# An adaLN block with sliding-window attention and a gated MLP: identity products in a row, another order of all engines' steps, and a last tile in three pieces

## The chip, the cores and the metric

The kernel runs on one core of a Trainium2 chip. The metric is device time in microseconds, from the launch to the end on that core. Engines in the views: PE (TensorE products), PEld (its weight loads), DVE (VectorE), ACT (ScalarE), POOL (GpSimd), SP (SyncE, which here only issues DMAs). Line numbers such as L1166 are those of the kernel before.

## The reference

The input x is 2048 rows of 448 values, in bfloat16. Six vectors of 448 come from one small product, and they shift, scale and gate two blocks:

```python
mod = (silu(c) @ w_mod).reshape(1, 6, 1, 448)
sa, ca, ga, sb, cb, gb = ...                       # six vectors of 448
h = layernorm(x) * (1 + ca) + sa
x = x + ga * A(h)                                  # attention, 16 heads of 28, window of 256 keys, softmax, then @ wo
h = layernorm(x) * (1 + cb) + sb
z = gelu(h @ w_in)                                 # 1792 wide: z1 and z2 of 896
g = w_sp @ layernorm(z2) + b_sp                    # a 2048 x 2048 product over the rows
x = x + gb * ((z1 * g) @ w_out)
```

## The kernel before

x lies in SBUF as 16 tiles of 128 rows (t or j, 0 to 15), worked on in quarters of four tiles (tb, 0 to 3). `hT` is the normalised activations transposed, so that features lie on partitions.

The work in its rough order of time:

- **Head.** Loads of x, c, the first part of w_mod and of wqkv; memsets; `ident`, a 128 x 128 identity made on POOL. `t_cT` (L517) turns c into a column, ACT applies silu. `t_mA` (L557, opened by one product at L561) is the modulation's first two vectors: three steps, each waiting for its own rows of w_mod (`t_wmA`, three loads, L412), 8, 16 and 8 products of one column each. `mod_out` (L569, L570) brings them to `modT`. The transposes of the first quarter (L708), their scaling with `modT` (L715 on ACT, L717 on DVE), and the Q and K products of the first quarter (L756) follow; L840 is V.
- **Identity products.** `warm` (L575 to L583) makes steps that multiply `ident` with itself into a free PSUM bank, 128 x 512, one product each. Nothing reads the result. Of the 54 steps that it offers, the order takes ten.
- **Attention**, tiles 0 to 15: scores (L942, L968, L977), exp on ACT (L929), masks on DVE (L984, L1004), the product with V (L1011), division (L1025, L1027), a DMA transpose, the product with wo (L1035; wo was multiplied with ga on POOL, L605), the residual (L1040), statistics (L621, L624, L626, L629, L633, L636), the second layer norm (`norm`, L641 on DVE or L646 on POOL, with a 64-column copy, L649 or L650), a DMA transpose to hT and its scaling (L1058, on ACT, DVE or POOL). For the quarters 2 and 3 the first layer norm goes the same way (L646, L692, L697 to L700); Q and K products of the quarters 1 to 3 are L798, their evictions L807 to L810, V's L843 to L846.
- **Gated MLP.** z2 (L1097) and z1 (L1143), gelu on ACT, layer norm of z2; the row product with w_sp (L1166, 28 groups of 16 products), a DVE step that adds b_sp (L1170), a POOL step that multiplies with z1 (L1173), the product with w_out (L1185), the residual (L1195), the store (L1200).

All of this is one list of steps. Each step names the engines that could run it, with a duration for each (for a product or a vector step, in us), what it depends on, and what buffer it takes. The order isn't computed when the kernel is built: `ORDER` (L19) is a written list of words such as `317.v` or `57.p.1` (step number, engine, buffer slot). `Sched.order` reads it: each engine executes its steps in the order of the list, and takes the engine and slot named there. The durations and landing times in the code, with `HOP`, `NEXT`, `PEL`, `SHAPE` and `TURN`, give only planned times; those decide in which sequence a step's semaphore waits are written (L234), and nothing else. `Sched.waits` then puts a semaphore wait ahead of each step for the dependences that its engine doesn't already know of; PE needs none for dependences on PE itself.

The step behind each word in the head of PE's queue: 46 is L517; 57 to 62 and 71 to 77 are identity products; 54, 55, 56 are the three steps of the modulation; 158 and 161 are L708; 170 is the first step of L756.

Of the kernel before, what the change touches and what calls it, by code (L numbers as in the profile page):

```python
# [9 lines left out]
HOP = 0.12  # L10

NEXT = {"dve": 0.08, "act": 0.11, "pool": 0.045}
# [7 lines left out]
2.a 25.v 35.g 0.s 26.v 27.v 28.v 38.g 39.g 3.a 4.s 36.g 45.a 33.g 29.v 5.s 30.v 31.v 37.g 32.v 40.g 6.s 7.s 41.g 8.s 140.v 141.v 57.p.1 58.p.2 46.p.0  # L20
48.a 47.a 59.p.3 60.p.4 54.p.1 61.p.5 62.p.6 55.p 34.g 142.g 49.a 56.p 134.v 135.v 136.v 143.g 137.g 138.g 144.v 145.a.0 139.a.1 71.p.7 72.p.3 158.p.2
50.g 126.a 127.v 111.v 112.v 159.v 161.p.3 160.a 162.a 163.a 128.g 42.g 1.s 9.s 10.s 130.a 131.g 11.s 12.s 13.s 14.s 15.s 16.s 152.v 129.v 153.v 154.v
146.v 155.g 132.v 147.v 148.v 149.g 133.g 156.v 73.p.0 74.p.6 170.p.4.5 171.p.6.7 172.p 173.p 174.p 175.p 178.p 176.p 177.p 184.p.0.1 185.p.2.3 186.p
187.p 188.p 189.p 193.p 179.p 192.p 181.a 182.a 150.v 151.v.2 197.v 157.a.3 183.a 167.p.5 164.p.6 191.p 218.p.3 190.p 168.v 169.a 195.a 165.v 166.v
194.v 200.p.7 226.v 230.v 227.v 219.a 180.a 196.a 204.a 201.p.5 198.p.6 202.v 232.v 231.v 228.v 229.v 233.v 53.v 205.a 199.p.1 203.a 378.p.0 209.p.0
220.p.7 224.p.6 206.p.1 379.a.0 384.p.0 225.a 44.g 51.g 213.v 52.v 43.g 234.g 235.g 210.a 385.a.1 207.p.0 211.a 221.a 380.v 382.v 236.v 239.g.0
237.v.1 113.p.1 238.v.2 115.v 240.v.3 114.v 403.p.0 117.p.0 388.v 118.v 244.p.1 208.p.6 404.a.2 405.a 212.a 245.v 386.v 241.p.0 410.p.0 222.p.7
381.p.0 383.p 214.s 217.s 216.s 215.s 17.s 24.s 20.s 18.s 22.s 120.s 119.s 21.s 19.s 246.a 242.v 243.v 411.a.3 249.p.1 223.a 412.a 250.a 247.p.0 248.a
430.p.0 432.p.0 387.p 389.p 431.a.4.0 275.v 279.v 281.v 277.v 282.v 280.v 278.v 276.v 283.g 326.v 284.g 390.v 391.v.0 285.v 332.v 413.v 406.v 408.v
287.v.0 415.v 434.v 288.g.1 292.s 291.s 253.p.1 261.p.0 254.a 438.p.0 262.a 439.a.5.1 265.p.1 407.p.0 259.p.0 409.p 266.a 260.a 459.p.0 460.a.6.2  # L30
433.a 251.p.1 414.p 267.p.0 416.p 467.p.0 468.a.0.3 328.v 289.v.2 293.s 286.v.3 330.v 252.v 435.v 290.s 268.v 417.v 418.v.1 329.v 263.p.1 440.p.0
273.p.0 441.a 264.a 257.s 256.s 121.s 258.s 255.s 392.s 419.s 436.p.0 488.p.0 464.v 333.v 327.v 331.v 442.v 443.v 489.a.1.4 437.p 444.p 271.p.1
461.p.0 445.p 463.v 334.g 471.v 274.v 446.v 447.v.2 272.v 462.a 296.a 294.g 297.g 295.g 335.g 496.p.0 497.a.2.0 269.p.0 469.p.0 465.p.0 466.p 298.p.1
470.a 517.p.0 299.a 270.v 336.v 493.v 500.v 490.p.0 300.p.0 473.p 316.p.1 472.v 492.v 301.v 518.a.3.1 521.v 317.v 491.a 525.p.0 498.p.0 474.p
526.a.4.2 475.v 476.v.0 530.v 340.v.0 529.v 501.v 522.v 124.g 337.g.1 125.g 339.g.2 122.g 338.g.3 123.g 448.s 341.s 343.s 342.s 477.s 344.s 318.p.0
312.p.1 494.p.0 319.a 313.a 499.a 546.p.0 302.p.0 519.p.0 495.p 420.p.1 502.p 547.a.5.3 554.p.0 520.a 555.a.6.4 303.v 551.v 421.v 503.p 527.p.0
304.p.0 310.p.1 504.v 505.v.1 559.v 558.v 422.v 305.a 528.a 575.p.0 576.a.0.0 393.p.0 548.p.0 523.p.0 524.p 531.p 532.p 583.p.0 394.v 550.v 345.v
533.v 580.v 534.v.2 549.a 311.a 584.a.1.1 314.p.0 315.v 478.p.1 556.p.0 552.p.0 479.v 346.v 116.s 306.s 506.s 309.s 307.s 535.s 308.s 557.a 604.p.0
449.p.0 553.p 560.p 561.p 577.p.0 605.a.2.2 578.a 612.p.0 613.a.3.3 423.v 588.v 587.v 579.v 450.v 562.v 507.p.1 585.p.0 480.v 395.v 563.v.0 508.v
347.g 348.g 324.p.0 581.p.0 325.a 586.a 633.p.0 634.a.4.4 351.p.1 606.p.0 320.p.0 582.p 607.a 321.a 641.p.0 642.a.5.0 608.v 509.v 609.v 396.v 451.v  # L40
452.v 481.v 397.g 453.g 398.g 482.g 454.g 510.v 617.v 424.v 352.v 589.p 590.p 614.p.0 591.v 536.p.0 616.v 322.p.1 537.v 592.v.1 646.v 511.v 399.v
637.v 400.v.0 401.g 455.g 425.g 615.a 323.a 662.p.0 663.a.6.1 355.p.0 610.p.0 635.p.0 611.p 618.p 619.p 636.a 356.v 670.p.0 671.a.0.2 538.v 620.v
638.v 621.v.2 349.p.1 643.p.0 353.p.0 639.p.0 644.a 350.a 691.p.0 564.s 402.s 666.v 645.v 675.v 622.s 593.s 692.a.1.3 664.p.0 640.p 647.p 648.p
# [224 lines left out]
def bass_adaLN_cond__sliding_block__mixer_gmlp__prompt_kernel(  # L268
# [111 lines left out]
    bM = View(banks, [(6,), (7,)])  # L380
    bA = View(banks, [(6,), (7,), (0,), (1,), (2,), (3,), (4,), (5,)])
    bF = View(banks, [(0, 1), (2, 3), (4, 5), (6, 7)])
    bG = View(banks, [(b,) for b in range(8)])
    MMS = 512 / 2400.0 + 0.003
    MMD = 448 / 2400.0 + 0.003
    PEL = 0.2


    dsem = []

    def load(name, eng, mb, fn, deps=(), prio=0.0, land=None, least=2.9):
        dsem.append(name)
# [876 lines left out]
```

## Time and profile before

| | |
|---|---|
| median of 3 runs | 276.64 us (275.81 to 276.93) |
| the profiled execution | 277.14 us, of which the span of its instructions is 275.2 us |
| busy, PE / DVE / ACT / POOL | 264.7 / 159.3 / 138.2 / 117.6 us |
| L1166, the product with w_sp, on PE | 97.3 us in 437 recorded products |
| L984, masks on DVE | 38.7 us, 56 of 0.723 us |
| L929, exp on ACT, the 2048-wide form | 53.2 us, 28 of 1.900 us |
| L646, layer-norm scaling on POOL / L641, the same on DVE | 1.103 / 0.433 us each |
| DMA | 26.41 MB in 66386 packets |

[...] A few product records are missing in the trace, which can look like a gap of one product's spacing.

### The profile page before, as it was taken

The numbers are of one execution on the slowest core, as the hardware profiler recorded it, in microseconds if no ns is written. First come the engines' busy times: TensorE is split into PE (matmuls) and PEld (weight loads), VectorE is DVE, ScalarE is ACT, GpSimd is POOL, SyncE is SP. The second block draws the span as 40 slices with busy tenths as digits, with TensorE's granted clock in tenths as the row PEclk, the third lists the DMA queues.
The fourth block names the chain that finished last, engine by engine and source line by source line (L and its number), as shares of the span: only waits on it lengthen the run. The fifth ranks groups of instructions, "written<-read, shape, count | busy, mean of one in ns | idle before, by whom it ended". The sixth has DMA issues, their size and how long they took to land.

```text
span 275.2 us, 7464 instructions
## 1 busy us (share of the span) xinstructions
PE 264.7 (96%) x3221; PEld 143.6 (52%) x3246; DVE 159.3 (58%) x370; ACT 138.2 (50%) x189; POOL 117.6 (43%) x172
## 2 busy tenths in 40 slices
PE   5999999899999999999999999999999999999995
PEld 1766565566676866445444444444444444444552
DVE  5599999999999999779365202100331042233343
ACT  5689999899998999889998400000000000000000
POOL 8531229720364694364799105000853053425110
PEclk9999999999999999999999999999999999999999
DMA  7958953551156746937999999100000000002022
GB/s 204 288 190 202 306 104 74 68 77 37 21 61 114 111 67 103 172 60 114 175 196 187 187 198 204 44 0 0 2 0 0 0 2 0 0 0 86 16 92 76
DMA packets 66386, 26.41 MB, mean 96 GB/s; under 512 B 56881, under 2 KB 65266, under 8 KB 66354
## 3 DMA queue, kind: packets, MB, share of 16 engines
q1 hardware_dynamic: 66080, 25.48, 46.7%
q8 instruction: 25, 0.41, 0.6%
q10 hardware_dynamic: 274, 0.46, 0.5%
q14 instruction: 7, 0.06, 0.1%
HBM read 9.07 MB, written 1.84 MB: 40 GB/s over the span
## 4 chain that ended last, share of the span: by engine, by line
PE 77%; DVE 9%; POOL 4%; DMA 4%; issue 2%; SPq 2%; ACT 2%; POOLq 0%
PE ps L1166 35%; PE ps L1097 8%; PE ps L1185 8%; PE ps L1143 8%; PE ps L1011 4%; PE ps L1035 3%; PE ps L968 3%; DVE PT L984 2%; DMA x_sb<-in_A_x_dram 2%; PE ps L756 2%; PE ps L840 2%; POOL xn L646 2%; DMA wmod<-in_w_mod_dram 2%; POOL wo_g L605 1%; DVE st_all L621 1%
## 5 line engine op out<-in xcount | busy, mean ns | idle before, releaser
L929 ACT ACTIVATE PW<-ps 128x2048 bf16<-128x2048 f32 (+1 forms) x56 | 67.5, 1260 | 4.1 <-PE ps L968 3.4
L1173 POOL TENSOR_TENSOR z1T<-tmpg,z1T 128x512 bf16<-128x512 bf16 x28 | 31.8, 1152 | 77.8 <-DVE tmpg L1170 77.8
L1170 DVE TENSOR_TENSOR tmpg<-ps,bsp_bc 128x512 bf16<-128x512 f32 x28 | 19.1, 690 | 73.9 <-PE ps L1166 48.7
L1166 PE MATMUL ps<-wspB,z 128*128 128x512 bf16 x217 | 49.0, 379 | 0.4
L1166 PE MATMUL ps<-wspA,z 128*128 128x512 bf16 x220 | 48.3, 379 | 0.3 <-issue 0.2
L984 DVE TENSOR_TENSOR PT<-PW,mask 128x1024 bf16<-128x1024 bf16 x56 | 38.7, 723 | 0.1
L1166 PEld LDWEIGHTS ps<-wspA,z 128*128 128x128 bf16 x224 | 21.8, 98 | 26.6 <-issue 0.4
L1166 PEld LDWEIGHTS ps<-wspB,z 128*128 128x128 bf16 x224 | 21.9, 98 | 26.1
L1011 PEld LDWEIGHTS ps<-Vaug,PT 128*128 128x128 bf16 x496 | 22.3, 96 | 4.4 <-DVE o_sb L1027 0.5
L1011 PE MATMUL ps<-Vaug,PT 128*128 128x32 bf16 x496 | 24.4, 177 | 0.1
L629 POOL TENSOR_TENSOR rs_all<-ve_all,neghalf 128x1 f32<-128x1 f32 (+1 forms) x31 | 20.0, 650 | 9.3 <-DVE ve_all L626 8.7
L1185 PE MATMUL ps<-w_out_g,z1T 128*128 128x448 bf16 (+1 forms) x119 | 22.3, 341 | 0.0
L1097 PE MATMUL ps<-w_in,hT 64*128 64x448 bf16 x224 | 22.2, 349 | 0.1
L1143 PE MATMUL ps<-hT,w_in 64*128 64x512 bf16 x196 | 21.8, 376 | 0.0
L1011 PE MATMUL ps<-Vaug,PW 128*128 128x32 bf16 x224 | 20.4, 176 | 0.0
L1195 DVE TENSOR_TENSOR fin<-ps,x_sb 128x448 bf16<-128x448 f32 (+1 forms) x17 | 9.8, 593 | 17.2 <-PE ps L1185 17.2
L621 DVE BATCH_NORM_STATS2 st_all<-x_sb 128x6 f32<-128x448 bf16 x32 | 19.1, 613 | 0.5 <-DMA x_sb<-in_A_x_dram 0.5
L798 PE MATMUL ps<-hT,WQK 128*128 128x512 bf16 x66 | 17.2, 379 | 2.1 <-DVE rec_all L1025 0.7
L1011 PEld LDWEIGHTS ps<-Vaug,PW 128*128 128x128 bf16 x224 | 17.6, 96 | 2.4
L626 POOL TENSOR_SCALAR ve_all<-mv_all 128x1 f32<-128x1 f32 (+1 forms) x16 | 4.8, 297 | 31.5 <-DVE mv_all L624 30.9
L1185 PEld LDWEIGHTS ps<-w_out_g,z1T 128*128 128x128 bf16 x119 | 11.6, 98 | 10.0
L1151 ACT ACTIVATE z1T<-ps 128x512 bf16<-128x512 f32 x28 | 14.5, 608 | 4.2 <-PE ps L1143 4.0
(125 smaller groups left out, 370.6 us busy)
## 6 DMA issues: line engine op xcount, KB each, us to landing
out_dram<-fin SPq DMA_DIRECT2D x15, 112.0 KB, 1.7
x_sb<-in_A_x_dram SPq DMA_DIRECT2D x3, 448.0 KB, 5.8
wmod<-in_w_mod_dram SPq DMA_DIRECT2D x1, 1344.0 KB, 9.0
w_in<-in_B_w_in_dram SPq DMA_DIRECT2D x1, 1344.0 KB, 7.7
QBD<-qT SPq DMA_DIRECT2D x16, 64.0 KB, 2.2
w_out_g<-in_B_w_out_dram SPq DMA_DIRECT2D x1, 784.0 KB, 5.8
bsp_bc<-in_B_b_sp_dram SPq DMA_DIRECT2D x1, 512.0 KB, 4.6
x_sb<-in_A_x_dram SPq DMA_DIRECT2D x2, 224.0 KB, 3.9
```

The costliest lines, as they stand in the source:

```text
L621: st = [dve(0.62 if True else 0, lambda e, t=t, ci=ci, s=s: e.bn_stats(st_all[:, slot, t, ci, :], s()), deps(t), prio) for ci, s in enumer ...
L629: rs = pool(0.41 + 0.155 * len(tiles), lambda e: e.tensor_tensor(rs_all[:, slot, a:b], ve_all[:, slot, a:b], neghalf[:, 0:b - a], ALU.pow) ...
L798: m = pe(4 * MMS, [lambda e, h=h, g=g, kc=kc, tb=tb: e.matmul(ps[:, h.slot[0], :], lhsT=WQK[:, kc, 4 * g:4 * g + 4, :].rearrange("p a b -> ...
L929: ex = act(xdur, lambda e, out_ap=out_ap, in_ap=in_ap: e.activation(out_ap(), in_ap(), ACT.Exp, scale=SCALE), [s], v - 8.0 + u, takes, tab ...
L984: return dve(0.70, lambda e: e.tensor_tensor(cols(hp.slot[0] * 2048 + 1024 * k, [[256, 4], [128, 2], [1, 128]]), cols(at_w() + 128 + 192 * ...
L1011: fns.append(lambda e, hp=hp, hO=hO, hi=hi, bi=bi, kb=kb, hd=hd, nb=nb, a=at[hi][bi], p_of=p_of: e.matmul(ps[:, hO.slot[0], 32 * hd:32 * h ...
L1097: return lambda e, kc, p0, start, stop: e.matmul(ps[:, hs[t % 2].slot[hf], 0:D], lhsT=hT[p0:p0 + 64, kc, t * 128:(t + 1) * 128], rhs=w_in[ ...
L1143: return lambda e, kc, p0, start, stop: e.matmul(ps[:, hs[b // 2].slot[b % 2], :], lhsT=w_in[p0:p0 + 64, kc, ft * 128:(ft + 1) * 128], rhs ...
L1166: m = pe(16 * MMS, [lambda e, h=h, si=si, ft=ft, tb=tb: e.matmul(ps[:, h.slot[0], :], lhsT=z2[:, si, ft * 128:(ft + 1) * 128], rhs=(wspA i ...
L1170: a = dve(0.7, lambda e, h=h, ht=ht, tb=tb: e.tensor_tensor(tmpg[:, ht.slot[0], :], ps[:, h.slot[0], :], bsp_bc[:, tb * 512:(tb + 1) * 512 ...
L1173: u = pool(1.16, lambda e, ht=ht, ft=ft, tb=tb: e.tensor_tensor(z1T[tb][:, ft, :], tmpg[:, ht.slot[0], :], z1T[tb][:, ft, :], ALU.mult), [ ...
L1185: return [lambda e, ft=ft: e.matmul(ps[:, h.slot[0], c0:c1], lhsT=z1T[t // 4][:, ft, (t % 4) * 128:(t % 4 + 1) * 128], rhs=w_out_g[:, ft, ...
```

## The change

Four things are changed in the text:

1. `ORDER` is another list. It has 1191 words for 1184. All steps of before are in it; new are three more identity products (75, 76, 77) and four steps of the new last piece (1228 to 1231). Steps per engine: PE 340 to 345, DVE 370 to 356, ACT 172 to 170, POOL 168 to 185, SP 134 to 135.
2. The planned durations, distances and landing times are others (`HOP`, `PEL`, `NEXT`, `land`, `tail` and the like). They change no instruction.
3. The last tile (15) is written in three pieces of 224, 112 and 112 columns, instead of two of 224.
4. The last tile's first product step names all earlier w_out products as dependences (`others`). These are PE steps too, so no wait comes of it.

PE's queue up to the first Q product, in words of the list:

```
before: 57 58 46 59 60 54 61 62 55 56 71 72 158 161 73 74 170 171 ...
after:  46 57 58 59 60 61 62 54 55 56 71 72 73 161 158 74 75 76 77 170 171 ...
```

The end of the list:

```
before: ... 1112.p 1175.p | DVE ... 1185 1179 1113 1176 | SP ... 1186 1180 1114 1177
after:  ... 1175.p 1220.p 1221.p 1224.p 1225.p 1228.p 1229.p | DVE ... 1185 1176 1226 1230 1222 | SP ... 1177 1227 1231 1223
```

(1220 to 1223 are the first piece of tile 15: six products, one product, the residual, the store; 1224 to 1227 the second, 1228 to 1231 the third. 1175 to 1177 are tile 8.)

The diff, with the list and most of the durations left out:

```diff
-HOP = 0.12
+HOP = 0.055
-NEXT = {"dve": 0.08, "act": 0.11, "pool": 0.045}
+NEXT = {"dve": 0.08, "act": 0.12, "pool": 0.045}
...
 ORDER = """
-2.a 25.v 35.g 0.s 26.v ... 57.p.1 58.p.2 46.p.0 ...
+... 57.p.2 58.p.3 59.p.4 60.p.5 61.p.6 62.p.7 54.p.1 55.p 56.p 144.g 145.a.0 50.a ... 71.p.0 72.p.3 73.p.4 161.p.2 158.p.3 ...
...
-    PEL = 0.2
+    PEL = 0.34
...
-    t_c = load("d_c", "act", 0.01, lambda e: e.dma_start(c_row[:], c[0:1, :]), prio=-98.98, land=2.9)
+    t_c = load("d_c", "act", 0.01, lambda e: e.dma_start(c_row[:], c[0:1, :]), prio=-98.98, land=1.6, least=1.5)
...
-        op = add({"pe": (dur, fns)}, deps, prio, take, lat=PEL)
+        op = add({"pe": (dur, fns)}, deps, prio, take, lat=0.2 if shape == "rows32" else PEL)
...
+    others = []
...
-            for c0, c1 in ((0, D // 2), (D // 2, D)) if t == NT - 1 else ((0, D),):
+            for c0, c1 in ((0, D // 2), (D // 2, 3 * D // 4), (3 * D // 4, D)) if t == NT - 1 else ((0, D),):
...
-                m = pe(k * one_mm, outs_of(range(k)), [us[:k], t_woutg], v + 0.01 * (c0 > 0), [h])
+                m = pe(k * one_mm, outs_of(range(k)), [us[:k], t_woutg] + (others if t == NT - 1 else []), v + 0.0001 * c0, [h])
                 if k < 7:
-                    m = pe(one_mm, outs_of([6]), [us, m], v + 0.05 + 0.01 * (c0 > 0))
+                    m = pe(one_mm, outs_of([6]), [us, m], v + 0.02 + 0.0001 * c0)
                 hf = Hold(fiR)
+                others.append(m)
```

More of the change, by code (lines that the diff above doesn't have):

```diff
@@ L420, in bass_adaLN_cond__sliding_block__mixer_gmlp__prompt_kernel @@
     LO, HI, BOTH = slice(0, D), slice(D, 2 * D), slice(0, 2 * D)
[L421 to L423 removed]
+    t_c = load("d_c", "act", 0.01, lambda e: e.dma_start(c_row[:], c[0:1, :]), prio=-98.98, land=1.6, least=1.5)
+    t_wmA = [head("d_wmAa", "act", wmod, w_mod, 0, 2, BOTH, -98.97, 5.0, least=4.2), head("d_wmAb", "sp", wmod, w_mod, 2, 1, BOTH, -98.97, 4.1, least=3.4),
+             head("d_wmAc", "sp", wmod, w_mod, 3, 64, BOTH, -98.96, 5.5, least=3.8)]
     t_wq = []
[L425 removed]
+    for k, (n, cols, at) in enumerate((("q", LO, (5.8, 6.6, 6.8)), ("k", HI, (8.1, 8.9, 9.1)))):
         a, b, c_ = [head("d_w%s%s" % (n, p), "sp", wq_st, A_wqkv, first, rows, cols, -98.95 + 0.03 * k + 0.004 * i, at[i], (), 3.9)
```

159 lines of the change are left out of this document (78 added, 81 removed).

## The prediction

> **What bounds the kernel now.** I read the page first, then the table of stretches, the chain and waits of TensorE, the timeline of the first 20 us, and at last the end.
>
> ```profile
> PE 264.7 (96%) x3221; PEld 143.6 (52%) x3246; DVE 159.3 (58%) x370; ACT 138.2 (50%) x189; POOL 117.6 (43%) x172
> PE   5999999899999999999999999999999999999995
> DVE  5599999999999999779365202100331042233343
> ```
>
> PE has work in nearly every slice; DVE is as full until about 108 us. The stretches put numbers to it (columns: us, then busy time and instructions of PE, PEld, DVE, ACT, POOL; clock; DMA share; GB/s):
>
> ```profile
> 0.00:10.00 10.00, 6.69 (x55) 3.07 (x56) 5.24 (x19) 5.21 (x9) 7.43 (x20) 1.00 0.86 235
> ...
> 18.00:50.00 32.00, 30.67 (x619) 18.65 (x625) 30.44 (x73) 31.34 (x38) 14.55 (x16) 1.00 0.73 156
> 50.00:54.00 4.00, 3.20 (x69) 2.16 (x72) 3.97 (x6) 3.38 (x6) 3.65 (x3) 1.00 0.34 64
> 54.00:108.00 54.00, 53.13 (x1400) 36.79 (x1403) 53.47 (x118) 50.56 (x51) 24.45 (x40) 1.00 0.46 71
> 108.00:154.00 46.00, 45.81 (x456) 21.77 (x458) 31.49 (x93) 38.77 (x70) 30.22 (x58) 1.00 0.90 153
> 154.00:272.00 118.00, 117.32 (x556) 55.24 (x565) 27.83 (x45) 2.99 (x6) 33.67 (x30) 1.00 0.21 47
> ```
>
> From 18 to 154 us PE idles 1.33 + 0.80 + 0.87 + 0.19 = 3.19 of 136 us. PE's useful work is the same before and after the change, so the end can move only by what happens before PE's first useful product, by these 3.19 us or new ones like them, and by the 3.2 us behind PE's last product. Two waits are more than a third of the 3.19:
>
> ```profile
> 50.23 0.81 PE L798 MATMUL ps<-hT,WQK 128*128 128x512 bf16 x3 [0.74 <-DVE rec_all L1025]
> ...
> 53.70 0.93 PE L1035 MATMUL ps<-wo_g,hT 128*128 128x448 bf16 x4 [0.42 <-POOL wo_g L605]
> ```
>
> The first waits for a bank that a busy DVE empties late, the second for the last of four scalings of wo on POOL. Now the head:
>
> ```profile
> 2.39 1.03 PE L578 MATMUL ps<-ident 128*128 128x512 bf16 x2 [2.39 <-POOL ident L498]
> 3.36 0.37 PE L517 MATMUL ps<-one,c_row 1*128 1x1 bf16 x4
> 3.66 1.04 PE L578 MATMUL ps<-ident 128*128 128x512 bf16 x2
> 5.62 0.19 PE L561 MATMUL ps<-xn,ident 128*128 128x8 bf16 x1 [0.92 <-DMA wmod<-in_w_mod_dram]
> ...
> 6.87 0.93 PE L557 MATMUL ps<-sc_sb,wmod 128*128 128x1 bf16 x24
> 7.66 1.01 PE L578 MATMUL ps<-ident 128*128 128x512 bf16 x2
> 8.47 1.06 PE L708 MATMUL ps<-ident,xn 128*128 128x128 bf16 x8
> ```
>
> The ten identity products (L578) lie in pairs between the steps that are needed. Their spacing is 0.427 us, against 0.216 for the same shape later (L1166): the clock is low here. It rises at about 11.58 us, inside the first useful products (by L756 alone):
>
> ```profile
> 10.17:11.46 1.29, 1.28 (x7) 0.91 (x7) 1.00 0.75 192
> 11.62:14.04 2.42, 2.42 (x25) 2.15 (x22) 1.00 1.01 328
> ```
>
> Seven starts in 1.28 us are 0.213 apart; behind 11.6 they are 0.109 apart. (The clock column's 1.00 is no record here.)
>
> **Part 1, the head.** Before: pair, L517, pair, L561 with the first eight of L557, pair, the rest of L557, pair, L708, pair, L756. After: L517 first, then six identity products in a row, all of the modulation, three, L708, four, L756: thirteen for ten. I walk it with the landings of this trace. ident is ready at 2.39; c_row has landed by then (landing record 2.08), so L517 goes ahead at next to no cost. Six products take 2.56 us, to about 4.95. The modulation still waits for its weights: 5.62, then the 6.87 at which the next part landed, then a third that ends at 7.66, since the loads and their queues stand as before. So PE now idles about 0.7 + 1.0 us where one pair used to fill the second gap; nothing needed is later by that. DVE's modT step, which stood behind a WQK copy until 8.64, can go at about 7.85, but that is hidden: PE has 7 identity products queued between 7.66 and L756. With the low clock: 7.66 + 3 x 0.427 + 0.85 (L708) + 4 x 0.427 = 11.5 for the first L756 product, against 10.18. The products needed for it (hT by DVE and ACT, two at 9.4 and 9.8 plus 0.4 to 0.6 each) are ready by 11.1. If the clock rises at 11.58 again, the seven products that ran low now run full, 7 x 0.104 = 0.70 back. Net +1.33 - 0.70 = **+0.63**. The two ends: the clock is up before 7.7 (then L756 starts at 9.6 at full rate, 10.18 + 0.70 - 9.61 = **-1.27**), or it rises later (below).
>
> [...]
>
> **Part 2, the order from 18 to 154 us.** The new constants issue nothing; they gave another order. Counting steps that change engines up to the modulation of hT, at the page's means: layer-norm scalings, net four from DVE (0.433) to POOL (1.103), DVE -1.73, POOL +4.41; hT scalings of L1058, DVE -3 x 0.439, ACT -0.80, POOL +3.99; those of L697, ACT +0.82, POOL -1.03; clearing QBD, DVE -0.91, ACT +1.06; evictions, seven ACT to DVE and four back, DVE +1.85, ACT -1.99; small steps, DVE -0.54, POOL +1.37. Sum: DVE **-2.65**, ACT -0.91, POOL **+8.74** us. DVE idles only about 2 us of 18 to 108, POOL about half of it, so the load goes where room is. What is worth anything is PE's 3.19 us. The eviction that the 0.74 waited for (the last K group of the third quarter) moves from DVE, where masks stand ahead of it, to ACT. The first L1035 stands 17 PE steps further back (step 127 instead of 110), several us of work, while POOL reaches the last wo scaling at about 53 by my count of its queue: the 0.42 goes. I take 0.74 + 0.42 = **-1.1** after rounding; what is late next is the many 0.1 us waits on masks, which I leave. Ends: -2.5 (all but a fifth of 3.19) and +1.5 (the last rival). On SP, x's last quarter is loaded directly behind the third (it lands at 28.9 now, released DVE's stats after a 0.5 us wait), part of wo goes behind the copies of q, hidden since POOL takes it up at 47 or later. From 154 us on, PE has 118 us of queued products, last weights land before (150.8 by the landing records, 154 needed), and one more wspB transpose ahead of them is offset by a wspA transpose issued earlier: nothing.
>
> **Part 3, the end.** Now a full-width tile is last: PE, then 0.62 on DVE, 0.03, SP's issue of 0.33, landing.
>
> ```profile
> 271.95 0.62 DVE L1195 TENSOR_TENSOR fin<-ps,x_sb 128x448 bf16<-128x448 f32 x1 [0.70 <-PE ps L1185]
> ```
>
> After, tile 15 is last in 224 + 112 + 112 columns. The wait list `others` is PE on PE and costs no semaphore. PE streams the same columns. But DVE's order is second piece, third piece, then the first and widest. Widths 448 and 224 cost 0.625 and 0.392, so 112 is estimated at 0.28: the third starts 0.2 behind the last product as now, the first starts 0.19 later and ends at 0.2 + 0.19 + 0.39 = 0.78, against 0.2 + 0.625 = 0.83. SP issues three transfers of 0.33 in line with that. Half the bytes in the last one: **0**, ends -0.2 and +0.2.
>
> **Sum.** +0.63 - 1.1 + 0 = -0.5. The profiled execution took 277.14 (span 275.2 and 1.94 around it) and would be 276.6; the median of the three runs is 276.64, so I say **276.1**. The spread of those runs (275.81 to 276.93) is what a clock rising 2 us earlier or later makes.
>
> **The rivals.**
> - *The row raises the clock early*, before L756 and its seven identity products. For: 2.56 us without a gap, where before no stretch that long came ahead of 5.62. Against: nearly 1.7 us of idling follows. 276.64 - 1.27 - 1.1 = 274.3.
> - *The clock rises later.* It rose 5.96 us after PE's last wait ended (5.62); that distance from 6.87 gives 12.8, and each us of low clock costs half: +0.6. 276.7. [...]
> - *POOL's scalings become the wait* (slower). In the third quarter three of the four scalings are on POOL in series, 3 x 1.103 = 3.3 us, where one was; the transposes to hT come behind the last. Before, hT was complete at 43.1 and PE's L798 took it at 43.9, so only 0.8 us is spare. For: that spare is small. Against: of the three hT scalings that POOL did then (3.07 us) two go to DVE. It decides once DVE gives POOL its statistics about a us later than the 31.6 I count; then PE stalls by 1.5, and the gain of part 2 is spent: 276.64 + 0.63 + 1.5 = 278.8.
>
> **How the numbers follow.** Forecast 0.36, early clock 0.30, late clock 0.12, POOL 0.22. Half a per cent, 1.4 us, is about what a measurement of this kernel can tell from no change. Faster by more: 0.28 of the early clock and 0.04 of the forecast's lower part, 0.32. Slower by more: 0.20 of the POOL case and 0.02 of late clock, 0.22. Same: 0.46. The range for 8 in 10 runs from just below the early clock's 274.3 to 278.5; the forecast's own is 275.2 to 277.3.
>
> **What would show it.** Right: thirteen L578 products, six from about 2.4; L557's second part still waiting until its landing; L756 starting between 9.6 and 11.5 and its spacing telling the clock; no PE wait over 0.3 us at 50 and 54; DVE's last step 224 wide. Wrong: idle of PE between 18 and 154 above 3.2 us, an L798 that waits for hT near 44, or a PE queue that ends with more than 3.3 us to go.

## The result, and the profile after

| | before | after |
|---|---|---|
| median | 276.64 us, 5 runs (275.81 to 276.93) | 280.82 us, 5 runs (280.22 to 281.23) |
| profiled execution, span | 277.14, 275.2 us | 280.22, 278.5 us |

The ratio is 1.0153 (95% interval 1.0134 to 1.0172): slower by about 4.2 us. The prediction was 276.1 us with a range to 278.5, so it was wrong, and in sign. (Two more runs of before have come to the three given above; the median is the same.)

The busy times of the page, to be read against those of before: PE has 35 products more on record (ten are really new, 25 were missing in the trace of before), DVE 2.7 us less, POOL 7.6 us more.

```profile
PE 267.7 (96%) x3256; PEld 144.7 (52%) x3256; DVE 156.6 (56%) x356; ACT 138.1 (50%) x187; POOL 125.2 (45%) x189
```

So the work moved from DVE to POOL as the prediction counted. The table of stretches (us, then busy time and instructions of PE, PEld, DVE, ACT, POOL; clock; DMA share; GB/s) says what it did to PE:

```profile
18.00:50.00 32.00, 30.61 (x622) 18.27 (x620) 29.55 (x71) 30.53 (x35) 12.17 (x13) 1.00 0.66 145
50.00:54.00 4.00, 3.42 (x84) 1.97 (x86) 4.00 (x5) 2.24 (x3) 3.90 (x3) 1.00 0.50 97
54.00:108.00 54.00, 53.41 (x1378) 36.18 (x1377) 52.88 (x111) 50.51 (x50) 28.16 (x45) 1.00 0.40 65
108.00:154.00 46.00, 45.27 (x470) 22.17 (x468) 28.66 (x82) 39.05 (x69) 35.52 (x72) 1.00 0.90 157
154.00:158.00 4.00, 2.00 (x17) 0.74 (x13) 0.94 (x2) 2.56 (x5) 2.27 (x3) 1.00 0.99 180
```

PE idles 1.39 + 0.58 + 0.59 + 0.73 + 2.00 = 5.29 us of these 140, against 3.25 of the same 140 in before (3.19 up to 154). The single waits, from PE's timeline (start, length, what, and in brackets the idle time ahead of it with its releaser):

```profile
49.62 0.93 PE L840 MATMUL ps<-wv,hT 128*128 128x448 bf16 x4 [1.13 <-DVE qT L809]
52.45 0.19 PE L1011 MATMUL ps<-Vaug,PT 128*128 128x32 bf16 x1 [0.45 <-DVE o_sb L1027]
55.10 1.04 PE L798 MATMUL ps<-hT,WQK 128*128 128x512 bf16 x4 [0.59 <-DVE qT L809]
157.30 0.39 PE L1167 MATMUL ps<-wspA,z 128*128 128x512 bf16 x1 [2.00 <-DVE z L1134]
```

(In the kernel after, L1166, L1170, L1173, L1185 and L1195 of before are L1167, L1171, L1174, L1186 and L1197.) The two waits that the prediction wanted gone, at 50.23 and 53.70, are gone. Three others on DVE stand in their place, and a wait of 2.0 us has appeared where before had none, ahead of the product with w_sp.

The best account is by five stretches of PE, cut at the starts of first products: to the first L942; from there to the first L1097 (attention); to the first L1166 (z, the gated MLP's input); to the last product (gating); and from there to the end of the span. Profiled executions, us:

| | head | attention | z | gating | end |
|---|---|---|---|---|---|
| before | 17.66 | 90.44 | 45.75 | 117.71 | 3.64 |
| after | 16.53 | 92.96 | 47.81 | 117.88 | 3.33 |
| difference | -1.13 | +2.52 | +2.06 | +0.17 | -0.31 |

(The first L1166 of before is missing in its record; its weight load puts it at 153.85, which the table uses.) The sum is +3.3 us, as the spans say. The loss is in two places, about half in each: attention and z.

The head of after, for the prediction's walk:

```profile
2.38 2.74 PE L578 MATMUL ps<-ident 128*128 128x512 bf16 x6
5.67 0.80 PE L557 MATMUL ps<-sc_sb,wmod 128*128 128x1 bf16 x24 [0.32 <-DMA wmod<-in_w_mod_dram]
10.12 2.07 PE L756 MATMUL ps<-hT,WQK 128*128 128x256 bf16 x16
```

The row is there, and the second part of L557 waits for its landing, as said. But that landing came at 5.67, not at 6.87, and L756 began at 10.12, with the full clock 0.3 us later (granted clock 1 from 10.44 by the clock's own record; 11.58 in before).

### The profile page after: what moved, and what is told of

It is laid out like the page before. It is cut to its first block, busy times and chain, and to the rows that moved or that the text cites. A ratio compares the mean times of both kernels' runs of the same rounds, so it can differ in the third digit from the quotient of the medians.

```text
span 278.5 us, 7512 instructions
## 1 busy us (share of the span) xinstructions
PE 267.7 (96%) x3256; PEld 144.7 (52%) x3256; DVE 156.6 (56%) x356; ACT 138.1 (50%) x187; POOL 125.2 (45%) x189
## 4 chain that ended last, share of the span: by engine, by line
PE 80%; POOL 7%; DVE 6%; ACT 2%; DMA 2%; issue 1%; ACTq 0%; DVEq 0%
PE ps L1167 35%; PE ps L1186 8%; PE ps L1097 7%; PE ps L1011 6%; PE ps L1035 4%; PE ps L968 4%; PE ps L840 4%; PE ps L798 4%; PE ps L756 3%; PE ps L977 2%; POOL rs_all L629 2%; DVE PT L984 2%; POOL z L1112 2%; ACT PW L929 2%; DMA wmod<-in_w_mod_dram 2%; POOL w_out_g L1051 1%
## 5 line engine op out<-in xcount | busy, mean ns | idle before, releaser
L1174 POOL TENSOR_TENSOR z1T<-tmpg,z1T 128x512 bf16<-128x512 bf16 x28 | 31.8, 1153 | 80.0 <-DVE tmpg L1171 80.0
L1171 DVE TENSOR_TENSOR tmpg<-ps,bsp_bc 128x512 bf16<-128x512 f32 x28 | 18.8, 690 | 78.7 <-PE ps L1167 72.5
L1167 PE MATMUL ps<-wspA,z 128*128 128x512 bf16 x224 | 48.8, 380 | 2.0 <-DVE z L1134 2.0
L1167 PE MATMUL ps<-wspB,z 128*128 128x512 bf16 x224 | 49.3, 380 | 0.0
L984 DVE TENSOR_TENSOR PT<-PW,mask 128x1024 bf16<-128x1024 bf16 x56 | 41.2, 760 | 1.1 <-ACT PW L929 1.1
L1167 PEld LDWEIGHTS ps<-wspA,z 128*128 128x128 bf16 x224 | 21.8, 98 | 28.7 <-DVE z L1134 2.5
L1167 PEld LDWEIGHTS ps<-wspB,z 128*128 128x128 bf16 x224 | 21.9, 98 | 26.3
L1011 PE MATMUL ps<-Vaug,PT 128*128 128x32 bf16 x496 | 25.0, 177 | 1.3 <-DVE PT L984 0.5
L1097 PE MATMUL ps<-w_in,hT 64*128 64x448 bf16 x224 | 22.2, 350 | 0.2 <-ACT PW L929 0.2
L1186 PE MATMUL ps<-w_out_g,z1T 128*128 128x448 bf16 (+2 forms) x126 | 21.9, 332 | 0.0
L1143 PE MATMUL ps<-hT,w_in 64*128 64x512 bf16 x196 | 21.8, 376 | 0.0
L798 PE MATMUL ps<-hT,WQK 128*128 128x512 bf16 x80 | 20.3, 380 | 0.6 <-DVE qT L809 0.6
L646 POOL TENSOR_SCALAR xn<-x_sb,rs_all,ve_all 128x448 bf16<-128x448 bf16 x17 | 14.8, 876 | 9.0 <-DVE ve_all L633 7.9
L1186 PEld LDWEIGHTS ps<-w_out_g,z1T 128*128 128x128 bf16 x126 | 11.7, 98 | 10.0
L1097 PEld LDWEIGHTS ps<-w_in,hT 64*128 64x128 bf16 x224 | 10.8, 94 | 10.8 <-issue 0.7
```

What stands on the lines that cost most here:

```text
L798: m = pe(4 * MMS, [lambda e, h=h, g=g, kc=kc, tb=tb: e.matmul(ps[:, h.slot[0], :], lhsT=WQK[:, kc, 4 * g:4 * g + 4, :].rearrange("p a b -> ...
L984: return dve(0.68, lambda e: e.tensor_tensor(cols(hp.slot[0] * 2048 + 1024 * k, [[256, 4], [128, 2], [1, 128]]), cols(at_w() + 128 + 192 * ...
L1011: fns.append(lambda e, hp=hp, hO=hO, hi=hi, bi=bi, kb=kb, hd=hd, nb=nb, a=at[hi][bi], p_of=p_of: e.matmul(ps[:, hO.slot[0], 32 * hd:32 * h ...
L1097: return lambda e, kc, p0, start, stop: e.matmul(ps[:, hs[t % 2].slot[hf], 0:D], lhsT=hT[p0:p0 + 64, kc, t * 128:(t + 1) * 128], rhs=w_in[ ...
L1143: return lambda e, kc, p0, start, stop: e.matmul(ps[:, hs[b // 2].slot[b % 2], :], lhsT=w_in[p0:p0 + 64, kc, ft * 128:(ft + 1) * 128], rhs ...
L1167: m = pe(16 * MMS, [lambda e, h=h, si=si, ft=ft, tb=tb: e.matmul(ps[:, h.slot[0], :], lhsT=z2[:, si, ft * 128:(ft + 1) * 128], rhs=(wspA i ...
```

## The experiments

Each "Measured" says which experiment it is, by its number; "the fifth experiment's kernel" is the kernel with that edit. Three theories stood at the start. **T1**: in z, POOL's queue brings the last z2 tile late. **T2**: in attention, evictions stand behind masks on a full DVE. **R1**: z is late only because attention was. The times of before that each ratio is taken against were run on the same chip (medians 276.7 to 277.2).

### Z: the scalings of w_out_g on POOL

POOL's queue at the end of z in after, and what DVE did last:

```profile
152.22 1.04 POOL L1051 TENSOR_TENSOR w_out_g<-w_out_g,gg_sb 128x448 bf16<-128x448 bf16 x1
153.36 0.27 POOL L636 TENSOR_SCALAR ve_all<-mv_all,rs_all 128x1 f32<-128x1 f32 x1
153.60 2.15 POOL L1112 TENSOR_SCALAR z<-z,rs_all,ve_all 128x896 bf16<-128x896 bf16 x2
155.72 0.55 POOL L629 TENSOR_TENSOR rs_all<-ve_all,neghalf 128x1 f32<-128x1 f32 x1
156.30 0.51 DVE L1115 TENSOR_SCALAR z<-z,mv_all,rs_all 128x896 bf16<-128x896 bf16 x1 [5.96 <-POOL rs_all L629]
```

POOL hardly idles here, and a scaling that nobody needs before the first L1186, at 233 us, stands ahead of z2's last steps. In before, two of the seven L1051 came after the first L1166 (at 169 and 198 us), and the last z2 step ended at 153.09, ahead of that product:

```profile
149.90 2.54 POOL L1112 TENSOR_SCALAR z<-z,rs_all,ve_all 128x896 bf16<-128x896 bf16 x2
152.60 0.49 DVE L1134 TENSOR_SCALAR z<-z,mv_all,rs_all 128x896 bf16<-128x896 bf16 x1
```

First experiment, the last four behind z2:

```diff
 # POOL's words in ORDER (836, 841, 838, 840 are L1051; 954 is the L629 at 155.72)
-836.g 994.g ... 901.g 841.g 919.g ... 973.g 838.g 902.g ... 1006.g 840.g 1007.g ... 954.g
+994.g ... 901.g 919.g ... 973.g 902.g ... 1006.g 1007.g ... 954.g 836.g 841.g 838.g 840.g
```

> Kernel after, with four of the seven L1051 scalings of w_out_g on POOL (1.0 us each) moved behind the last z2 step of POOL; nothing else is moved. Theory T1 (POOL's queue in the z phase, with these scalings between the small steps of z2, brings the last z2 tile late): PE's wait of 2.0 us ahead of the first L1167 product goes to below 0.3 us, and the time falls from 280.8 to 278.7. Rival R1 (the last z2 is late because PE, DVE and ACT brought its inputs late, by the waits at 49 to 55 us and at 108): the wait stays above 1.5 us and the time within 0.5 us of 280.8.

Measured (first): 280.12 us, ratio 1.0111 (1.0079 to 1.0142). The time gained 0.7 us, a third of what T1 said, and PE still waited 1.3 us. The stretch z is 47.15 us to the first product on record; the product ahead of it is missing, and by its weight load z is 46.91, 0.9 us less than in after. The timeline of DVE, and of POOL beside it, has the reason:

```profile
155.46 1.22 DVE L1115 TENSOR_SCALAR z<-z,mv_all,rs_all 128x896 bf16<-128x896 bf16 x1 [3.77 <-POOL rs_all L629]
156.60 1.22 DVE L1134 TENSOR_SCALAR z<-z,mv_all,rs_all 128x896 bf16<-128x896 bf16 x1
155.38 4.34 POOL L1051 TENSOR_TENSOR w_out_g<-w_out_g,gg_sb 128x448 bf16<-128x448 bf16 x4
```

DVE's last two steps, 0.51 us each in after, took 1.22 with POOL's scalings beside them. (The profile names ACT as PE's releaser there, but ACT's first eviction of that group had ended 0.45 us before; DVE's end at 157.82 is what PE's load at 157.90 followed.) So the scalings were moved once more, out of the way of both:

```diff
-... 954.g 836.g 841.g 838.g 840.g 1123.g 1090.g 1135.g 1129.g ...
+... 954.g 1123.g 836.g 1090.g 841.g 1135.g 838.g 1129.g 840.g ...    # 1123, 1090, 1135, 1129 are L1174
```

> Kernel after, with the same four L1051 scalings as in the first experiment, now each behind one of the first four L1174 products of POOL instead of in a row ahead of them. In the first experiment PE still waited 1.3 us ahead of L1167, and DVE's last two z2 steps (L1115, L1134) took 1.22 us each beside the scalings, against 0.51 alone in after. Theory T1b (POOL's queue and, beside it, POOL's scalings slowing DVE): the two DVE steps take 0.5 us again, PE's wait ahead of L1167 is below 0.3 us, and the time is 1.3 us under the first experiment's, about 278.8 (before 277.0). Rival (PE waited for ACT's evictions of the last L1143 bank, which the profile names as releaser): the wait stays at 1.3 us and the time at 280.1.

Measured (fifth): 279.19 us (276.98 to 281.00, 12 runs), ratio 1.0083 (1.0050 to 1.0117). DVE's last two steps:

```profile
153.62 0.51 DVE L1115 TENSOR_SCALAR z<-z,mv_all,rs_all 128x896 bf16<-128x896 bf16 x1 [3.77 <-POOL rs_all L629]
154.04 0.51 DVE L1134 TENSOR_SCALAR z<-z,mv_all,rs_all 128x896 bf16<-128x896 bf16 x1
```

The wait is gone. This trace lacks the first L1167 as that of before lacks the first L1166, and the stretch from L1097 to the first one on record is 45.97 us in both: all of the +2.06 is back. By the ratios, four places in one queue are worth 0.7% of the kernel. (That median lies between two groups of runs: in six of the twelve TensorE's mean granted clock was 0.988 to 0.994, and they average 280.46 us; the six at 0.999 or 1.0 average 278.11. The last section has more of this.) T1 holds in this wider form: POOL's place in the chain, and POOL's scalings beside DVE's.

Two kernels spliced from the two lists ask the same from the other side. The seam is at the first L1097:

```diff
-ORDER of before, all of it                 | -ORDER of after, all of it
+before to the first L1097, then after      | +after to the first L1097, then before
```

> The order of before up to the first L1097 product (head and attention), then the order of after for all that is left (z phase, gating, last tile in three pieces). If the z phase's order itself is late (T1), PE waits about 2 us ahead of L1167 and the time is 277.0 + 2.0 = 279.0. If after's z phase is late only because the attention ahead of it was (R1), it is 277.0.

> The order of after up to the first L1097 product (new head and attention), then the order of before for all that is left (z phase, gating, last tile in two pieces). The waits from 18 to 110 us cost PE about 4.2 us in the trace of after and 2.7 in that of before (starts of products, spacing beyond the usual): 277.0 + 1.5 = 278.5 by the theory that the two parts add up. If the waits of the attention are hidden behind a later common limit, 277.0; if all of after's loss comes through the attention, 281.2.

Measured (the two splices): 281.40 us, ratio 1.0174 (1.0146 to 1.0201), and 282.55 us, ratio 1.0203 (1.0179 to 1.0227). Both are spoilt by waits that neither list has: the first by 1.3 and 0.8 us for DVE ahead of L1097 and L1143, the second by 2.1 us for DVE ahead of L1143, because z follows an attention that it was not made for. Their stretches still speak: attention was 90.81 and 93.05 us, as in the list that it came from, and the first splice, with before's attention, waited for the last z2 just as after did (2.2 us, for DVE's L1134). R1 falls.

### Attention: evictions, masks and POOL

The second experiment puts three evictions back on ACT; the fourth does so together with the first experiment's edit.

> Kernel after, with three evictions of the third and fourth quarter that the change gave to DVE (two of L809, one of L845) put back on ACT at the places that they had before. Theory T2 (they stand behind masks on a full DVE and make PE wait at 49.6 and 55.1 us): the waits of 1.13 and 0.59 us go, PE's idle time from 18 to 108 us falls from 2.6 to about 1 us. If POOL alone sets the end of the z phase (T1), PE then only waits longer ahead of L1167, 2.0 + 1.6 = 3.6 us, and the time stays at 280.8; if the z phase just follows PE (R1), the time falls by 1.6 to 279.2. Rival: ACT is as full as DVE there, the evictions now wait behind its exponentials, and PE idles as much as before.

```diff
-... 338.v 501.v 521.v 522.v 299.v ...  493.v 529.v 305.v 319.v 530.v ...       # on DVE
+... 470.a 299.a 518.a ...  499.a 319.a ...  555.a 305.a 313.a ...              # on ACT, as in before
```

> Kernel after with both edits: the four w_out_g scalings behind the z2 steps, and the three evictions on ACT. T1 and T2 together: the two gains add up, 280.8 - 2.1 - 1.6 = 277.1, and this edit gains more on top of the evictions alone than it does on top of after. If only one of the two is the cause, the time is 278.7 (T1 alone) or 279.2 (T2 alone); if neither, 280.8.

Measured (second): 284.51 us, ratio 1.0258 (1.0236 to 1.0281), and together with the first experiment's edit (fourth) 284.42 us, ratio 1.0261 (1.0240 to 1.0282): by the ratios about 3 us worse than after. The rival held: PE now waited 2.9 us for one of the moved evictions behind ACT's exponentials, 1.6 us for L1027, and then the clock fell as well (last section), so part of the 3 us is the clock. Here, where DVE and ACT both are full, changing the engine of an eviction cured nothing.

What made DVE full? After has less for it to do. But the masks themselves were slower: the 54 masks (L984) between 18 and 108 us took 0.724 us on average in before and 0.763 in after. Sorted by what POOL did beside them: 0.67 and 0.68 us where POOL was idle all the time; 1.07 us (five masks) and 1.18 us (six masks) where it scaled wo (L605). POOL's and DVE's timelines of after:

```profile
46.95 4.36 POOL L605 TENSOR_TENSOR wo_g<-wo_g,gg_sb 128x448 bf16<-128x448 bf16 x3
52.42 1.48 POOL L605 TENSOR_TENSOR wo_g<-wo_g,gg_sb 128x448 bf16<-128x448 bf16 x1
46.44 2.53 DVE L984 TENSOR_TENSOR PT<-PW,mask 128x1024 bf16<-128x1024 bf16 x2 [0.57 <-ACT PW L929]
49.65 2.21 DVE L984 TENSOR_TENSOR PT<-PW,mask 128x1024 bf16<-128x1024 bf16 x2
52.32 2.13 DVE L984 TENSOR_TENSOR PT<-PW,mask 128x1024 bf16<-128x1024 bf16 x2
```

Two masks undisturbed take 1.28 us; these six took 6.87 instead of 3.84, and DVE is 3.0 us behind just where PE waits for it three times. In before the four scalings had one L646 each between them; the five masks beside them were slowed too, by 1.9 us together, between 48 and 55 us. **T3**: POOL's wo scalings take DVE's time there. To test it, the scalings were cut to one column, first on the fifth experiment's kernel, then on before:

```diff
-e.tensor_tensor(wo_g[:, kc, :], wo_g[:, kc, :], gg_sb[:, 0, :], ALU.mult)
+e.tensor_tensor(wo_g[:, kc, 0:1], wo_g[:, kc, 0:1], gg_sb[:, 0, 0:1], ALU.mult)
```

> The kernel of the fifth experiment (after, with the w_out_g scalings late), in which the four L605 scalings of wo on POOL work on one column of 448 only: the scaling of wo by the gate is left out for the rest. Theory T3 (POOL's scalings share something with DVE's masks: beside L605 a mask, L984, took 1.11 us in after, alone 0.68): the masks between 46 and 54 us fall to 0.7, the 49.6 us wait of PE from 1.3 to below 0.6, and the time by 1.5 to 2 us, from 279.2 to 277.5. Rival T2b (the waits come from where the evictions stand in DVE's queue, behind two or three masks): the waits lose at most what the masks ahead of them gain, 0.3 us each, and the time falls by 0.6 to 278.6.

> Kernel before, with the same cut of the four L605 scalings to one column (the rest of that scaling is left out). PE's waits of before at 50.0 (0.69 us beyond the spacing) and 53.7 (0.57, for the last of these scalings): the second goes by any theory. By T3 the first goes too and the time is 277.0 - 1.2 = 275.8; by T2b the first stays and it is 276.4.

Measured (sixth), on the fifth experiment's kernel: 276.95 us, ratio 0.9986 (0.9961 to 1.0011), 2.2 us less by the medians and 2.7 by the ratios, with attention at 90.59 us (93.04 in the fifth) and one wait of 0.29 us left of the three. Measured (seventh), on before: 275.53 us, ratio 0.9936 (0.9911 to 0.9960), a gain of 1.65 us by the medians and 1.8 by the ratios; PE's wait of 0.42 is gone and that of 0.74 is 0.2. So before paid for these scalings too, and what they cost more in after is 0.6 to 0.9 us by these times. By the profiles it is about 1.2 us: 2.45 against some 1.2. (The seventh's attention is 90.67 us, with a wait of 1.49 us at 32.57, behind steps of DVE that stood until x's last quarter was there at 29.58; before has no such wait. Without it 89.2, an estimate, against 90.44.) The rival, that the place of the evictions in DVE's queue is what counts, was tried by itself:

```diff
 # DVE's words (299, 305: L809; 475, 476: L1025, L1027; 501 to 529, 819: masks; 658: L633)
-... 501.v 521.v 522.v 299.v 475.v 500.v 492.v 476.v 493.v 529.v 305.v ... 820.v 658.v 819.v
+... 501.v 299.v 521.v 522.v 475.v 476.v 500.v 492.v 305.v 493.v 529.v ... 820.v 819.v 658.v
```

> The kernel of the fifth experiment, with four steps moved in DVE's own queue and nothing else: the eviction that PE waited for at 49.6 us goes ahead of two masks, the o_sb product (L1027) directly behind its reciprocal as in before instead of behind two masks, the eviction awaited at 55.1 ahead of two masks, and a small L633 step behind the last mask. T2b: the three waits of 1.3, 0.6 and 0.6 us go and the time falls by about 2 us, 279.2 to 277.2. T3 alone: DVE's total is the same and so slow beside POOL that the masks, now later, make PE wait as long elsewhere: 279.2.

Measured (eighth): 278.66 us, ratio 1.0059 (1.0034 to 1.0084): 0.5 us of the 2 that T2 said. The three waits went, and PE's timeline has two others for the masks themselves:

```profile
53.14 0.19 PE L1011 MATMUL ps<-Vaug,PT 128*128 128x32 bf16 x1 [1.13 <-DVE PT L984]
54.34 0.19 PE L1011 MATMUL ps<-Vaug,PT 128*128 128x32 bf16 x1 [0.73 <-DVE PT L984]
```

T3 holds against T2: in another order DVE is as late, and other products wait. Leaving work out can't tell whether the work or its place costs, so the next kernels are whole. On the fifth experiment's kernel the four scalings were held until a later eviction:

```diff
-339.g 122.g 124.g 123.g 340.g 125.g         # POOL; 122 to 125 are L605, 339 and 340 L646
+339.g 340.g 122.g 124.g 123.g 125.g
+for k in (122, 123, 124, 125): sc.ops[k].deps.add(sc.ops[305])
```

> The kernel of the fifth experiment, whole, with the four L605 scalings of wo behind POOL's last layer-norm step of that stretch and held until the eviction that ends at 55.05 us in after; they then run at about 55 to 60 us, where PE waited for nothing in after, and the first product that needs them (L1035) starts at 60.8. By T3 (beside POOL's scalings the masks are slow, and that matters only where PE waits for DVE) nearly all of what leaving them out gained comes back with the whole computation: 279.2 - 2.0 = 277.2. If the price of a scaling beside masks is the same wherever it stands, PE waits at 56 to 62 us instead and it is 279.2.

Measured (tenth): 277.88 us, ratio 1.0030 (1.0013 to 1.0048): 1.3 us of the 2.2 by the medians, 1.5 of the 2.7 by the ratios, and in the profiles 1.20 of 2.45 (attention 91.84 us). The scalings ran from 51.9 to 57.3, three masks beside them took 4.12 us, and PE waited 1.04 us behind them at 57.3 in place of the three waits (0.28 is left of the first):

```profile
52.30 4.12 DVE L984 TENSOR_TENSOR PT<-PW,mask 128x1024 bf16<-128x1024 bf16 x3
```

The place is about half of what the scalings cost. On before, the scalings were put at 54 us in the same way, with the first L1035 steps behind them:

```diff
-... 310.p 575.p 393.p ... 314.p 478.p 556.p 552.p ... 604.p 577.p 449.p     # 420, 393, 478, 449 are L1035
+... 310.p 575.p ... 314.p 420.p 556.p 552.p 393.p ... 604.p 478.p ... 577.p 449.p
```

> Kernel before, whole, with the four L605 scalings on POOL held until the L809 eviction that ends at 55.4 us, and the first four L1035 products and their L1040 steps moved some 3 to 7 us later to stand behind them. Leaving the scalings out gained 1.65 us on this kernel; if the place is what counts, this gains about 1.3: 275.7, below both kernels. If L1035 was a filler that PE now misses at 53.7 and 58.2, or waits for the scalings at 61, it gains nothing: 277.2 or more.

Measured (eleventh): 278.30 us, ratio 1.0034 (1.0013 to 1.0055). PE, without these products to fill in, waited for ACT's exponentials (0.9 us) and for DVE's division (0.8 us) at 53 to 69 us: the rival held. The last experiment puts before's scalings in a row, as after has them, and changes nothing else:

```diff
-124.g 337.g 125.g 339.g 122.g 338.g 123.g      # POOL; 337, 339, 338 are L646
+124.g 125.g 122.g 123.g 337.g 339.g 338.g
```

> Kernel before, whole, with POOL's four L605 scalings of wo in a row from 44.1 us, ahead of the three L646 steps that stood between them (44.1 to about 48.5 instead of 44.1 to 53.6). PE's wait for the last scaling at 53.7 (0.57 us beyond the spacing) goes by any theory, and no scaling is left beside the masks at 48 to 54 us, where PE waited 0.69 at 50.0. By T3 both waits go, as far as the masks at 44 to 48 us have room: 277.0 - 1.2 = 275.8, below both kernels. If the masks at 44 to 48, now slowed, only move the wait to 47 to 49 us, as in after, where three scalings in a row stood there: 277.0 or more.

Measured (fourteenth): 279.01 us, ratio 1.0081 (1.0058 to 1.0104). The wait for the last scaling did go, and the median is 2.3 us higher. POOL's row of scalings, and the four masks that DVE did beside it:

```profile
43.94 4.93 POOL L605 TENSOR_TENSOR wo_g<-wo_g,gg_sb 128x448 bf16<-128x448 bf16 x4
44.91 5.10 DVE L984 TENSOR_TENSOR PT<-PW,mask 128x1024 bf16<-128x1024 bf16 x4
```

The same four masks in before:

```profile
45.05 2.84 DVE L984 TENSOR_TENSOR PT<-PW,mask 128x1024 bf16<-128x1024 bf16 x4
```

5.10 - 2.84 = 2.26 us on DVE. PE waits 1.40 us for a mask and 0.74 for the eviction behind it, and attention takes 91.99 us, 1.55 more than in before. The rest of the median's 2.3 goes with a lower clock: the profiled run, at the full clock, took 278.37 us, and the five others, 278.62 to 279.52, had a mean granted clock of 0.992 or 0.993 (last section). My expectation was the wrong way round; the other outcome that it names, "as in after", is what came. One re-ordering of POOL's queue, with no other change, makes 1.55 us of loss on before, where after's attention has 2.52.

What is left of after's attention, waits of PE at 108 to 109 us (0.66 and 0.37 us beyond the usual spacing), was not found:

```diff
-... 740.v 711.v 820.v 658.v 819.v ...          # on the tenth experiment's kernel; 740, 711: L1040
+... 820.v 658.v 819.v 740.v 711.v ...
```

> The tenth experiment's kernel, with the two L1040 steps of DVE that stand ahead of the last two masks moved behind them. In after PE waits 0.66 and 0.37 us beyond the spacing at 108 to 109 us, in before 0.26 and 0.25. If the place of these two steps is the reason, the time is 0.5 under the tenth experiment's; if it is ACT's exponentials or POOL beside the masks there, the same.

Measured (twelfth): 277.70 us, ratio 1.0029 (1.0005 to 1.0052), the waits unchanged. The two L1040 steps are not their cause.

### Head and tail by themselves

The third experiment is the row alone, on before.

> Kernel before, with the row alone: six identity products behind L517, all of the modulation, three, L708, four, then L756 (thirteen for ten). DVE, ACT, POOL and SP are those of before. If the row brings the full clock earlier with L756 starting as before (as the trace of after shows: 0.57 us earlier while L756 started 0.05 us earlier), the time is 276.64 - 0.6 = 276.0. If the row costs what the prediction said (+0.63), it is 277.3. If the landings of the loads set the head whatever stands between them, it is 276.6.

```diff
-57 58 46 59 60 54 61 62 55 56 71 72 158 161 73 74 170          # PE's words, ten identity products
+46 57 58 59 60 61 62 54 55 56 71 72 73 158 161 74 75 76 77 170 # thirteen
```

Measured (third): 277.46 us (276.18 to 280.01, 12 runs), ratio 1.0016 (0.9993 to 1.0040). The reverse edit on the eighth experiment's kernel (pairs for the row):

> The kernel of the eighth experiment, with the head's identity products in five pairs between the steps as before (ten for thirteen). If the row costs nothing, the same time as the eighth; by the row on before (+0.4, within its uncertainty) 0.4 less; if the row raises the clock early in most runs, 1 us more.

Measured (ninth): 278.76 us, ratio 1.0066 (1.0037 to 1.0095), against 1.0059 with the row. The row's price lies between -0.2 and +1.1 us on before and is not to be seen here. Nor is it in the profiles: the first L942 starts at 17.2 us on average in the eleven kernels with the row, and at 17.2 in the seven with pairs (16.0 to 18.0 and 16.3 to 18.0).

> The order of before up to the last 55 us, then the tail of after: tile 15 last, in pieces of 224, 112 and 112 columns. By the prediction nothing (277.0, within 0.3). Rival (a tile whose products all wait for the seventh gated row leaves PE idle at the end, or three issues on SP cost more than one): above 277.5. The other way, the narrower last step on DVE and the shorter last transfer bring 0.3 or more: below 276.7.

The edit is a splice again: before's list up to the last 55 us, then after's. Measured (third splice): 277.49 us, ratio 1.0036 (1.0014 to 1.0057). Its profile has a wait of 0.85 us between L1186 products at 266 us, for the last gated row from POOL, that after does not have: one of the products that fill in there in after stands further ahead in before's list. The tail's own price is read better from the stretches above: products +0.17 us, end -0.31. All other kernels here with after's list in the gating stretch have 117.65 us there from the first product on record, all with before's 117.49.

## Why the prediction was wrong

**Part 1, the head: order right, size not to be told.** Thirteen products, L517 first at no cost, PE idle until the landing and no new wait on the path: all as walked. +0.63 lies inside what the row on before measured. In the profiled run the head was 1.13 us shorter instead, but kernels with before's head show first L942 products at 16.30 to 18.00 us, so this is the run's own landing and clock, not the row. The walk took one run's landing of 6.87 us as fixed; it was 5.67 in the next.

**The early and the late clock.** In kernels with the row the granted clock rose at 5.6 to 5.8 us in three profiles, at 10 to 12 in the others; in one of the three it fell again at 9.08 and rose at 12.49. With five pairs it rose at 9.7 to 12.6. So the early clock exists, but where it stayed PE then waited 0.8 and 0.9 us at 12 us for a layer-norm step of DVE (L641), and the first L942 still started at 16.0 and 16.1, 0.2 to 0.3 us ahead of the earliest without it. The prediction held the idling behind the row against an early clock. In these three profiles the row and the products behind it ran from 2.4 to about 5.4 us, 3.0 us, then PE idled for 0.7 to 1.6 us, and the clock was up before PE went on. The 12.8 us of the late clock was an estimate from a single distance, 5.96 us from the end of PE's last wait to the rise; in after it was 4.77 (5.67 to 10.44).

What the three have in common can be read from the clock's own record. Where the clock changes again later in a profile, the change comes 3.41 us, or a whole multiple of it, after the one before: 3.41 in the second splice, 44.37 = 13 x 3.413 from rise to fall in the second, fourth and eighth experiments, and 262.83 = 77 x 3.413 in before and 269.65 = 79 x 3.413 in after, from the rise to the fall behind the last product. Counted back by 3.41 from the rise, the stretch ahead of it began at 2.23 to 2.36 in the three, ahead of the row's first product (2.39 to 2.42), and held the whole row. In the other eight kernels with the row such a stretch began or ended inside it (at 3.1 to 5.0), and the clock rose later. So the early clock came where such a stretch happened to begin just ahead of the row, in three profiles of eleven. Whether a row does better there than pairs has one case to go by: in the eleventh experiment, with pairs, the stretch from 2.40 to 5.81 held six identity products too, but for a few hundredths of a us, in three pairs, and the clock rose at 12.64.

**Part 2, the order: this is the step that failed.** The sentence was "DVE idles only about 2 us of 18 to 108, POOL about half of it, so the load goes where room is". The counts were right: DVE's work fell, POOL's rose. The step from there to the time was not. Room on POOL was not free while DVE ran: what POOL did there came back as slower masks, 3.0 us of them between 46 and 54, where before had 1.9 us between 48 and 55. The term was -1.1, from two waits that vanish; both did, and the stretch measured **+2.5**: DVE was later in just that place, and three new waits took theirs. Of the +2.5 the experiments tie about 1.2 us to POOL's scalings of wo and their place (the tenth, and the sixth against the seventh); the rest was not found. The trace of before held the row that says so: the masks at 51.71 to 54.8 us took 3.09 us for three, where three undisturbed take 1.9, and the wait for wo_g at 53.70 was read as a scaling that comes late, not as a scaling that makes others late. One of the two waits was also smaller than its row. The L798 row at 50.23 says x3, and this step has four products, as its weight loads do:

```profile
49.99 0.55 PEld L798 LDWEIGHTS ps<-hT,WQK 128*128 128x128 bf16 x4 [0.95 <-DVE KT L809]
```

By them the first product ran at 50.01, unrecorded, so 0.52 us of the 0.74 were idle.

**"From 154 us on ... nothing".** The prediction checked the weights (landed well before) and never walked POOL's queue through z, though its own table had POOL at 30.22 of 46 us there and rising. The term was 0 and the stretch z measured **+2.06**; moving four scalings in POOL's queue took all of it back, as the fifth experiment shows.

**Part 3, the end.** 0 with ends at 0.2: +0.17 - 0.31 = -0.14. Right.

**The rival "POOL's scalings become the wait"** had the right engine and the right sign, at half the size (278.8 us is 2.2 more than before, and it was 4.2), but the wrong scalings and the wrong way. There is no L798 wait for hT near 44 us; in attention it was not POOL's result that came late but DVE's, beside POOL. Of the signs named as "wrong", the idle time of PE showed, though barely where it was to be looked for: 3.29 us from 18 to 154, against the 3.2 named; the wait of 2.0 us lies behind 154.

**The sum that would have been right**: attention +2.5, z +2.1, the rest within a few tenths. With the z scalings late and the wo scalings held back the ratio goes 1.0153, 1.0083, 1.0030, which is 3.4 of the 4.2 us; some of that is the lower clock that half of the fifth experiment's runs had and none of the tenth's. The profiles of these three, without such a fall, give 2.06 for z and 1.20 for attention. What stays open is the other 1.3 us of attention: the waits at 108 to 109, the masks beside the scalings at 52 to 57, and what the change did to attention apart from POOL's scalings. No whole kernel here was faster than before.

## What to carry to other kernels

Before work is moved from a full engine to an idle one, sort the full engine's instructions by what the idle one does beside them: if they are slower there, the move is paid for by the engine that it was to relieve, and here most of all when the moved steps stood in a row (1.55 us of attention for four scalings in the fourteenth). Walk every queue through the stretch behind a change, up to the point where all of its results are needed at once, even if no instruction there was added. And count the products of a step (x3 of four) before a gap is called a wait.

## What the runs showed of the hardware

**POOL and DVE slowed each other.** Beside POOL's scalings of wo (L605) a mask (L984) took 1.07 (before) and 1.18 us (after) on average, at most 1.5, instead of 0.68, beside those of w_out_g (L1051, first experiment) a z2 step (L1115, L1134) 1.22 instead of 0.51, and POOL's own L605 beside masks 1.46 to 1.49 instead of 1.04. Three steps that read PSUM kept their time: in before L809 took 0.68 and L1027 0.62 beside L605 (one of each), and 0.68 and 0.62 with POOL idle, and L1170 took 0.69, in eleven beside L1173 as in sixteen with no product of POOL beside them. Why some steps were slowed and others not, no run here shows.

**The clock fell in the middle of kernels in which PE never idled for long.** In the eighth experiment, behind the two waits of 1.13 and 0.73 us shown above, the table of stretches has (us, busy times, clock, DMA share, GB/s):

```profile
50.00:55.10 5.10, 3.23 (x78) 1.79 (x76) 5.07 (x8) 3.21 (x5) 5.10 (x4) 1.00 0.42 82
55.20:58.50 3.30, 2.97 (x46) 1.47 (x45) 2.74 (x5) 2.84 (x4) 0.00 (x0) 0.50 0.52 91
58.60:62.00 3.40, 3.24 (x91) 2.33 (x91) 2.42 (x6) 2.16 (x3) 2.94 (x3) 1.00 0.36 96
```

The granted clock was 0.5 from 55.13 to 58.55, 3.41 us, and the run 280.41 us against a median of 278.66. In the second and fourth experiments, with waits of 1.6 and 2.9 us, it was 0.5 for twice as long, 6.83 us, and their runs all lay between 283.65 and 284.69 us. What makes the clock fall was not shown. It is not the length of a wait alone: after's wait of 2.00 us, up to 157.30, has no fall behind it, while the eighth experiment's two, 1.13 and 0.73 us, have one. Nor is it PE's share of busy time alone. In the 3.41 us that end where the clock fell, PE was 45% busy in the eighth experiment and 56% in the second. Counted on from its rise at 10.44 in steps of 3.413 us, after had such a stretch 44% busy, from 153.80 to 157.22 us, without a fall. Where a stretch begins may count here too, by one case: the ninth experiment has the eighth's two waits to 0.06 us, one of its stretches ends between them (at 52.30), and its profile shows no fall.

Other runs had such falls too, by the mean granted clock that is on record for each. It was 1.0 in after's five runs, 0.998 or more in all runs of before, and 0.999 or 1.0 in all of the sixth, tenth and twelfth experiments. It was 0.987 to 0.994 in six of the twelve runs of the fifth, of the eighth and of the ninth, and in five of the six of the fourteenth; one stretch of 3.41 us at half speed makes 0.994 (an estimate: 1 - 0.5 x 3.41 / 276). Such runs were 2.4 us longer on average in the fifth, 1.6 in the ninth and 0.2 in the eighth. Where in a run the clock fell is known for the profiled ones alone.
